# Linear attention and a gated MLP in one kernel: K and q of two steps transposed in 64x64 tiles, with a new order of all instructions

## The chip, the cores and the metric

One NeuronCore of a Trainium2 chip runs the whole program. The metric is the device time of one execution in microseconds (us); the median of several runs counts. The engines are TensorE (PE, with its weight loads listed apart as PEld), VectorE (DVE), ScalarE (ACT), GpSimd (POOL) and SyncE (SP, which here only issues DMAs). Each works through its own queue in order and waits on semaphores for the others.

## The reference

Two stages follow each other. The first is attention with a decay per head, in blocks of 64 positions, with a 64x64 state per head; the second is a gated MLP whose gate mixes positions.

```python
# q, k, v: (4, 8, 768, 64) float32; lam: (8,)
for b in range(12):                                   # blocks of 64 positions
    intra = (qb @ kb^T) * Dmask                       # Dmask[i, j] = lam ** (i - j) for i >= j, else 0
    out[:, :, sl] = intra @ vb + (qb * lam_pow) @ kv_state
    kv_state = lam ** 64 * kv_state + (kb * rev_pow)^T @ vb
x = out.transpose(0, 2, 1, 3).reshape(4, 768, 512)
h = relu(x @ w_in)                                    # w_in: (512, 1024)
u, v = h[..., :512], h[..., 512:]
v_n = (v - mean(v)) / sqrt(var(v) + 1e-6)             # over the 512 features
v_s = w_spatial @ v_n + b_spatial                     # over the 768 positions
y = (u * v_s) @ w_out                                 # (4, 768, 512) float32
```

## The kernel before

The work is cut into 12 steps; step n is 256 positions (two chunks c of 128) of batch n // 3, all 8 heads. The decay is put into k and q themselves: k is multiplied by lam to a power of the position (`lv`), q by the inverse power (`lqn`, or `lq` after the transpose), so the mask is of zeros and ones.

A step goes through these operations; each is a short function, and the name in brackets is its token in the order:

- loads of 512 KB each of q, k, v (LQ, LK, LV) on SP's queue; three buffers each (`q_in`, `k_in`, `v_in`), so the load of step n waits until step n-3 has used its buffer;
- k times its decay to bf16 (KM), q cast (QC) or scaled (QM), v cast (VC), into two buffers each (`kc`, `qc`, `vb`);
- the transposes of k and q, which the scores need with the 64 features on the partitions. Steps 0 to 4: on PE (TK, TQ: 128x128 tiles against an identity, eight for a whole step, into one PSUM bank), then a copy out of PSUM (EK) and a product with `lq` (EQ). Steps 5 to 11: DMA transposes on SP's queue (DK, DQ);
- scores (SC), the mask (MK, on DVE, the largest single group of DVE), the state (KV, or KS, which mixes the state's matmuls into half of the scores), the state's copy (SS), the product with v and the state (AV), the copy to `xT` (EX); SC, KV, KS and AV use 64x64 tiles of PE;
- the v half of w_in (PV), its relu (EV), the statistics (BN, RA, RD, NB), the normalised v (VN), the u half (PU) and its relu (EU); 128x128 tiles.

When the three steps of a batch are done, its gate follows: the bias is copied to a PSUM bank (GP), w_spatial times v_n is added (PW), the product with u is taken (GM), and w_out (PO, or PH for half of a tile's columns) gives the output, copied (EO, EH) and stored (ST, SH) by SP. w_spatial is transposed once on PE (WT, EW). The weights are loaded and cast by DMAs on POOL's queue: WI.0 and WI.1 (the v and the u half of w_in), WS.0 and WS.1 (w_spatial), WO (w_out). GT on POOL only reads one number of a load, so that what follows it on POOL waits for that load. FL are four matmuls of the identity with no result that is used; LB, LN, LL, LX and LT make the decays from `lam`.

PSUM has eight banks; bank 7 holds the state, the other seven are given out by the order. The order of everything is written out by hand in the string `ORDER`: each token is an operation, its arguments and its engine (T PE, D DVE, A ACT, P POOL, S SP). `TK.3.2.6.T` is the transpose of k of step 3, whole (2; 0 and 1 are halves), into bank 6. Each engine's queue is the tokens with its letter, in the order of the string, and semaphores are set for what reads and writes the same tile or bank:

```python
    with tc.manual_schedule():
        for token in ORDER.split():
            name, *args, e = token.split(".")
            ops[name](e, *map(int, args))
```

Lines of the profile: loads 192, KM and QM 286, casts and copies 177 (ACT), 179 (DVE), 181 (POOL), weights 248, 253 and 257, bias 260, GT 244, LN 210, LX 219 and 220, LT 224, TK and TQ 316, EQ 330, SC 347, MK 352, KV 364, KS 377 and 385, AV 406 and 415, PV 440, EV and EU 445 (ACT) and 447 (DVE), PU 488, WT 500, PW 514, GM 520, PO 525, PH 534, SH 544, ST 548, DMA transposes 299 (k) and 303 (q).

Of the kernel before, what the change touches and what calls it, by code (L numbers as in the profile page):

```python
# [21 lines left out]
FL.4.6.T MK.0.0.2.3.D TQ.2.0.2.T MK.1.1.0.1.D AV.0.0.3.6.T FN.0.3.6.A TQ.2.1.0.T SS.0.1.A MK.1.0.4.5.D LT.2.A
KM.2.0.P KV.1.0.T AV.1.0.1.4.T KM.2.1.D WS.1.P TK.2.0.5.T AV.0.1.3.6.T LV.2.S SS.1.0.D FN.1.1.4.A KV.1.1.T
LK.3.S EX.0.1.6.A AV.1.1.1.4.T BS.S LK.5.S EX.1.0.1.A EK.2.0.5.D LQ.3.S EX.0.0.3.D PV.0.1.5.T FL.15.6.T
EX.1.1.4.A WO.P TK.2.1.3.T GT.1.2.P PV.1.1.1.T EV.1.1.1.A EQ.2.1.0.D EQ.2.0.2.D VC.2.P WT.0.0.0.T EK.2.1.3.D
SC.2.0.2.3.T PV.1.0.4.T BN.1.1.D PV.0.0.6.T EW.0.0.0.A MK.2.0.2.3.D EV.0.1.5.A EV.1.0.4.A SC.2.1.0.1.T SS.1.1.A
PU.1.1.5.T BN.1.0.D WT.2.0.4.T KV.2.0.T MK.2.1.0.1.D RA.1.A BN.0.1.D LV.3.S AV.2.0.2.3.T EV.0.0.6.D SS.2.0.A
FN.2.2.3.D PU.1.0.0.T BN.0.0.D AV.2.1.2.3.T EX.2.1.3.D RD.1.D WT.1.0.1.T RA.0.A NB.1.D RD.0.D EX.2.0.2.A
EW.1.0.1.D EW.2.0.4.A NB.0.D VN.0.0.A WT.1.1.6.T KM.3.0.P EW.1.1.6.D KM.3.1.P VC.3.P WT.2.1.3.T PV.2.1.2.T
PV.2.0.1.T VN.1.0.A PU.2.1.4.T LK.4.S EV.2.0.1.A WT.0.1.6.T VN.1.1.A EV.2.1.2.D EU.1.0.0.A BN.2.0.D EU.1.1.5.A  # L30
BN.2.1.D VN.0.1.D LQ.4.S PU.2.0.2.T RA.2.A RD.2.D EW.0.1.6.A PU.0.0.1.T GP.0.0.0.0.A VN.2.1.D PU.0.1.5.T
# [5 lines left out]
GM.0.1.0.2.D EQ.4.2.5.D GM.0.0.1.1.D AV.3.0.3.6.T KM.5.1.P LK.6.S LV.5.S VC.4.A FN.3.3.6.D KS.4.0.4.5.T SS.4.0.A
GM.0.2.0.0.D SC.4.1.1.2.T AV.3.1.3.6.T KS.4.1.4.5.T QM.5.1.P PO.0.4.0.T QM.5.0.D MK.4.0.4.5.D EX.3.1.6.A
EX.3.0.3.A PO.0.5.6.T EO.0.4.0.A KM.6.0.D PV.3.0.3.T DK.5.S EV.3.0.3.A LQ.6.S MK.4.1.1.2.D PU.3.0.4.T PV.3.1.5.T
VC.5.P DQ.5.S KM.6.1.P GP.0.3.0.0.D PW.0.3.0.0.T QM.6.1.P AV.4.0.1.2.T SS.4.1.A EV.3.1.5.A LQ.7.S EO.0.5.6.A  # L40
BN.3.0.D FN.4.1.2.A DK.6.S LK.7.S EU.3.0.4.D LV.6.S QM.6.0.P KV.5.0.T SC.5.0.3.4.T SC.5.1.5.6.T AV.4.1.1.2.T
DQ.6.S GM.0.3.0.0.D EX.4.0.1.A PO.0.1.0.T PO.0.0.1.T SS.5.0.D MK.5.1.5.6.D MK.5.0.3.4.D LK.8.S EX.4.1.2.A
EO.0.0.1.D PV.4.0.5.T AV.5.0.2.6.T EV.4.0.5.A EO.0.1.0.D PV.4.1.3.T FN.5.2.6.D LQ.8.S EV.4.1.3.A AV.5.1.2.6.T
EX.5.1.6.A EX.5.0.2.A BN.3.1.D BN.4.0.D PO.0.3.4.T QM.7.0.P PU.4.1.1.T BN.4.1.D LV.7.S KM.7.0.P VC.6.D
PV.5.0.5.T RA.4.A EU.4.1.1.A PV.5.1.0.T KM.7.1.D PU.5.1.3.T RA.3.A RD.3.D EV.5.0.5.A RD.4.D EV.5.1.0.A BN.5.0.D
ST.0.1.S SC.6.1.1.2.T EO.0.3.4.A QM.7.1.P NB.3.D KS.6.0.5.6.T BN.5.1.D DK.7.S NB.4.D DQ.7.S PU.4.0.0.T SS.6.0.A
# [541 lines left out]
```

## Time and profile before

| | |
|---|---|
| time, median of 3 runs | 146.82 us (146.6 to 147.3) |
| the profiled execution | 147.23 us, its span 145.5 us |
| PE / PEld busy | 130.7 us (90%) / 84.2 us (58%) |
| DVE / ACT / POOL busy | 113.3 us (78%) / 81.1 us (56%) / 46.8 us (32%) |
| DMA | 32.28 MB, mean 222 GB/s over the span |
| chain that ended last | PE 61%, DMA 22%, POOL 4%, DVE 4% |

The span is what the profiler recorded from the first to the last instruction; the execution's own time is a little longer. Busy time of PE counts a matmul from its start to its modelled end, and matmuls overlap, so the cadence (start to start) is what a matmul costs when the next follows. The chain is followed back from the last instruction: at each step to what released it, or to the instruction before it on its engine. Rows of the timeline and of the chain give start, duration, engine, line of the program, operation and tiles; in brackets stands the idle time before and what ended it. Rows of the windows give for each stretch its length, the busy time and number of instructions of PE, PEld, DVE, ACT and POOL, the granted clock, the DMA share and GB/s.

### The profile page before, as it was taken

What the parts mean: (1) busy time and instruction counts of PE and PEld (TensorE: products, weight loads), DVE (VectorE), ACT (ScalarE), POOL (GpSimd) and SP (SyncE); (2) the same over time, 40 slices, a digit from 0 to 9 for tenths busy, and PEclk for the clock granted to TensorE, in tenths of its full rate; (3) what the DMA queues carried; (4) which work ended last, traced back from release to release, by engine and by line L of the source; (5) the groups of instructions that cost most, each with busy time, mean ns of one, the idle gap of its engine ahead of it and who ended that gap; (6) DMA issues with size and microseconds to landing.
All of it is one profiled execution on the core that took longest, in us unless ns stands there. A gap on an engine that the chain in (4) does not pass through costs nothing.

```text
span 145.5 us, 4623 instructions
## 1 busy us (share of the span) xinstructions
PE 130.7 (90%) x1938; PEld 84.2 (58%) x1954; DVE 113.3 (78%) x227; ACT 81.1 (56%) x161; POOL 46.8 (32%) x59
## 2 busy tenths in 40 slices
PE   1269999899999996999999999999999999999990
PEld 1147765578756655457765646766665644865630
DVE  2568975987899985978999988979789779877410
ACT  3775276669938553378954442979233235870151
POOL 7449910205058256331902494034110000000000
PEclk9999999999999999999999999999999999999999
DMA  3999999999999999999999999998933002715064
GB/s 88 346 347 347 228 214 216 216 236 335 295 250 347 220 202 264 299 192 358 176 299 179 347 343 248 192 330 257 192 83 138 5 0 93 272 75 213 0 258 177
DMA packets 58375, 32.28 MB, mean 222 GB/s; under 512 B 15858, under 2 KB 55282, under 8 KB 58354
## 3 DMA queue, kind: packets, MB, share of 16 engines
q1 hardware_dynamic: 55968, 29.23, 78.3%
q0 software_dynamic: 2384, 2.75, 10.8%
q8 instruction: 15, 0.25, 0.7%
q14 instruction: 6, 0.05, 0.1%
q10 hardware_dynamic: 2, 0.00, 0.0%
HBM read 24.77 MB, written 6.29 MB: 213 GB/s over the span
## 4 chain that ended last, share of the span: by engine, by line
PE 61%; DMA 22%; POOL 4%; DVE 4%; issue 2%; SPq 2%; ACT 2%; POOLq 0%
PE ps L514 17%; PE ps L525 13%; PE ps L488 11%; PE ps L440 10%; DMA k_in<-in_k_dram 9%; DMA win_sb<-in_moe_w_in_dram 8%; DMA qT<-qc 4%; PE ps L415 3%; PE ps L347 2%; SPq L192 2%; PE ps L406 2%; DVE a_sb L352 2%; POOL kc L286 2%; ACT vn L476 1%; POOL qc L181 1%
## 5 line engine op out<-in xcount | busy, mean ns | idle before, releaser
L514 PE MATMUL ps<-wt_sb,vn 128*128 128x384 bf16 x192 | 34.2, 326 | 0.0
L352 DVE TENSOR_TENSOR a_sb<-ps,m 128x1024 bf16<-128x1024 f32 x24 | 28.8, 1215 | 2.7 <-PE ps L406 1.3
L286 POOL TENSOR_TENSOR kc<-k_in,lv 128x512 bf16<-128x512 f32 x17 | 17.6, 1044 | 27.2 <-PE ps L377 11.7
L514 PEld LDWEIGHTS <-vn 128*128 128x128 bf16 x192 | 18.0, 98 | 11.5
L488 PE MATMUL ps<-xT,win_sb 128*128 128x256 bf16 x192 | 23.8, 273 | 0.8 <-DMA win_sb<-in_moe_w_in_dram 0.6
L440 PE MATMUL ps<-win_sb,xT 128*128 128x512 bf16 x91 | 22.9, 379 | 0.5 <-issue 0.2
L525 PE MATMUL ps<-wout_sb,gT 128*128 128x512 bf16 x81 | 21.3, 379 | 1.0 <-issue 0.5
L488 PEld LDWEIGHTS <-win_sb 128*128 128x128 bf16 x192 | 18.4, 98 | 5.5 <-DMA win_sb<-in_moe_w_in_dram 0.8
L520 DVE TENSOR_TENSOR gT<-ps,uT 128x384 bf16<-128x384 f32 x32 | 17.1, 549 | 4.3 <-PE ps L514 3.5
L455 DVE BATCH_NORM_STATS2 st<-vh 128x6 f32<-128x512 bf16 x24 | 16.3, 680 | 1.9 <-ACT vh L445 1.8
L177 ACT ACTIVATE o_sb<-ps 128x512 f32<-128x512 f32 (+1 forms) x19 | 10.7, 570 | 11.7 <-PE ps L525 11.2
L286 POOL TENSOR_TENSOR qc<-q_in,lqn 128x512 bf16<-128x512 f32 x12 | 12.4, 1046 | 11.8 <-DMA q_in<-in_q_dram 7.1
L445 ACT ACTIVATE vh<-ps 128x512 bf16<-128x512 f32 x17 | 10.1, 592 | 10.4 <-PE ps L440 10.3
L177 ACT ACTIVATE xT<-ps 128x512 bf16<-128x512 f32 x18 | 9.9, 596 | 9.7 <-PE ps L415 9.7
L440 PEld LDWEIGHTS <-xT 128*128 128x128 bf16 x96 | 8.9, 98 | 9.5 <-ACT xT L177 0.5
L525 PEld LDWEIGHTS <-gT 128*128 128x128 bf16 x92 | 8.4, 98 | 8.5
L181 POOL CAST vb<-v_in 128x1024 bf16<-128x1024 f32 x6 | 6.2, 1038 | 18.9 <-DMA v_in<-in_v_dram 13.7
L445 ACT ACTIVATE uT<-ps 128x512 bf16<-128x512 f32 x18 | 10.1, 592 | 0.9 <-PE ps L488 0.9
L415 PE MATMUL ps<-a_sb,vb 64*64 64x128 bf16 x384 | 10.5, 226 | 0.0
L177 ACT ACTIVATE ps<-bsp 128x384 f32<-128x384 f32 x18 | 8.6, 494 | 2.9 <-DVE a_sb L352 1.9
L347 PE MATMUL ps<-qT,kT 64*64 64x128 bf16 x288 | 8.2, 240 | 2.0 <-DMA qT<-qc 1.1
L476 ACT ACTIVATE vn<-vh,shift,rstd 128x512 bf16<-128x512 bf16 x11 | 8.5, 807 | 1.7 <-DVE shift L470 1.7
(77 smaller groups left out, 175.7 us busy)
## 6 DMA issues: line engine op xcount, KB each, us to landing
q_in<-in_q_dram SPq DMA_DIRECT2D x12, 512.0 KB, 6.0
k_in<-in_k_dram SPq DMA_DIRECT2D x12, 512.0 KB, 6.0
v_in<-in_v_dram SPq DMA_DIRECT2D x12, 512.0 KB, 6.0
out_dram<-o_sb SPq DMA_DIRECT2D x23, 256.0 KB, 2.4
wsp_raw<-in_moe_w_spatial_dram POOLq DMA_DIRECT2D x2, 576.0 KB, 12.8
win_sb<-in_moe_w_in_dram POOLq DMA_DIRECT2D x2, 512.0 KB, 10.8
wout_sb<-in_moe_w_out_dram POOLq DMA_DIRECT2D x1, 512.0 KB, 17.8
bsp<-in_moe_b_spatial_dram SPq DMA_DIRECT2D x1, 384.0 KB, 21.4
```

What stands on the lines that cost most here:

```text
L177: nc.scalar.activation(out=o, in_=i, func=AF.Copy)
L286: vec(e).tensor_tensor(out=dst[n % NCA][:, u].rearrange("p u m o d -> p o (u m) d"), in0=src[n % NIN].rearrange("p (o u) m d -> p o u m d" ...
L347: nc.tensor.matmul(out=pa[o][row(c), w, j], lhsT=kT[n % NTR][row(o), u, j, c * Q64:(c + 1) * Q64], rhs=qv(n, o, u, c), start=(w == 0 and j ...
L352: nc.vector.tensor_tensor(out=a_sb[n % NA][:, i].rearrange("p o w j x -> p o w (j x)"), in0=ps[:, b0:b1 + 1:b1 - b0].rearrange("p o (w y) ...
L415: nc.tensor.matmul(out=po[c ^ o][row(w), c, i], lhsT=vb[n % NCA][row(c), 4 * o + u, j, :], rhs=a[row(c), i, o, w, j, :], start=(r == 0 and ...
L440: nc.tensor.matmul(out=bank(b), lhsT=x[:, slot(c, g)], rhs=win_sb[:, g, DH:DFF], start=(g == 0), stop=(g == NCH - 1))
L445: nc.scalar.activation(out=o, in_=i, func=AF.Relu)
L455: nc.vector.bn_stats(out=st6[p2][:, t], in_=vh[p2][:, t])
L488: nc.tensor.matmul(out=pu[:, f2].rearrange("p (c x) -> p c x", c=2), lhsT=win_sb[:, g, f * P:(f + 1) * P], rhs=x[:, slot(0, g):slot(1, g) ...
L514: nc.tensor.matmul(out=bank(b)[:, 0:HW], lhsT=vn[bb % 2][:, s, f * P:(f + 1) * P], rhs=wt_sb[:, s, i * HW:(i + 1) * HW], start=False, stop ...
L520: nc.vector.tensor_tensor(out=gT[bb % 2][:, f, cols], in0=bank(b)[:, 0:HW], in1=uT[bb % 2][:, f, cols], op=ALU.mult)
L525: nc.tensor.matmul(out=bank(b), lhsT=gT[bb % 2][:, f, t * P:(t + 1) * P], rhs=wout_sb[:, f, :], start=(f == 0), stop=(f == NCH - 1))
```

## The change

K and q of steps 3 and 4 are transposed by one operation, TT, instead of TK and TQ: 64 transposes of 64x64 tiles, k first and then q. A tile of rows c goes to the first or second of two neighbouring banks, k to the first half of each bank, q to the second. FK copies k out of both banks with one instruction, FQ multiplies q out of both with `lq`. Steps 0 to 2 keep TK and TQ in halves, steps 5 to 11 the DMA transposes.

The order string is another one throughout: every queue has a new sequence, many operations another bank, some another engine (GP 26 on ACT and 6 on DVE, where 18 and 14 were; VN 8 and 16, where 11 and 13 were). There are three FL instead of two. The two half tiles of the output (PH, EH, SH) come after all other output tiles.

```diff
-LQ.0.S lam.A msk.P idn.P LK.0.S LQ.1.S mkc.D QC.0.1.D posk.P pos.P LB.0.T LN.0.A LL.D QC.0.0.P LK.1.S LX.A
-KM.0.1.D QC.1.0.D TQ.0.0.1.T KM.0.0.D LT.1.A LT.0.A TK.0.1.2.T TQ.0.1.3.T EQ.0.1.3.D KM.1.1.D TK.0.0.4.T LV.0.S
-KM.1.0.P EK.0.1.2.A EQ.0.0.1.D WI.0.P EK.0.0.4.D SC.0.1.5.6.T QC.1.1.P WS.0.P TQ.1.0.0.T LV.1.S VC.0.A
...
+pos.P msk.P lam.A LQ.1.S QC.1.0.A idn.P LK.0.S posk.P LK.1.S LQ.0.S QC.0.1.P LV.0.S GT.1.1.P mkc.D LB.0.T VC.0.P
+LN.0.A WI.0.P FL.16.1.T TQ.1.0.2.T LV.1.S QC.1.1.D LL.D LX.A LT.0.A FL.0.3.T KM.0.0.D TK.0.0.4.T EK.0.0.4.A
+KM.1.0.D TK.1.0.5.T KM.0.1.D TK.0.1.6.T EK.1.0.5.A TQ.1.1.1.T QC.0.0.D EK.0.1.6.A KM.1.1.D TQ.0.0.0.T TQ.0.1.3.T
+TK.1.1.4.T EQ.0.1.3.D SC.0.1.5.6.T EK.1.1.4.D LT.1.A EQ.1.1.1.D EQ.0.0.0.D KV.0.0.T SS.0.0.D LQ.2.S MK.0.1.5.6.D
+KV.0.1.T GT.1.2.P WS.0.P WI.1.P GT.2.1.P SC.0.0.3.4.T QC.2.1.P VC.1.A QC.2.0.A LK.2.S SS.0.1.A KM.2.1.P
...
+AV.1.1.3.4.T LV.2.S EX.1.1.4.A VC.2.P KV.2.0.T SC.2.0.5.6.T EX.1.0.3.D MK.2.0.5.6.D SS.2.0.D LK.3.S LQ.3.S
+PV.1.0.2.T PV.1.1.0.T EV.1.1.0.D SC.2.1.3.4.T MK.2.1.3.4.D PV.0.1.1.T BS.S EV.0.1.1.D WT.1.0.5.T WT.0.0.6.T
+PV.0.0.0.T AV.2.0.3.4.T BN.1.1.D WO.P PU.1.1.1.T LQ.4.S KM.3.1.P EW.1.0.5.A FN.2.3.4.D AV.2.1.3.4.T QC.3.2.P
...
-EU.0.1.5.A TK.3.2.6.T GP.0.2.1.5.A VN.2.0.D EU.0.0.1.A PW.0.0.0.0.T EW.2.1.3.D GT.2.1.P QC.3.2.D EU.2.1.4.A
-LV.4.S EK.3.2.6.D PW.0.2.1.5.T GP.0.1.1.1.A GM.0.0.0.0.D GP.0.3.1.4.A GP.0.2.0.0.A TQ.3.2.3.T PW.0.1.1.1.T
...
-MK.3.0.5.6.D TK.4.2.3.T KM.5.0.P GM.0.3.1.4.D PW.0.1.0.2.T LQ.5.S EK.4.2.3.A TQ.4.2.5.T PW.0.0.1.1.T
...
+WT.2.1.6.T EW.1.1.4.A EU.1.0.5.A RA.2.A PU.2.0.3.T EU.2.0.3.A TT.3.4.5.T EW.2.1.6.D VN.1.0.A VN.0.1.D
+GP.0.2.1.3.A RD.2.D EU.0.0.2.A VN.2.0.D VN.0.0.D VN.2.1.D KM.4.0.P EU.0.1.0.D PU.2.1.6.T EU.2.1.6.D GP.0.0.0.0.A
+PW.0.2.1.3.T PW.0.0.0.0.T FQ.3.4.5.D QC.4.2.D FK.3.4.5.A SC.3.1.4.5.T EU.1.1.1.A GM.0.2.1.3.D KS.3.0.1.2.T
+GP.0.1.1.6.A PW.0.1.1.6.T SS.3.0.D GP.0.3.1.3.A MK.3.1.4.5.D GT.2.2.P GM.0.1.1.6.D KS.3.1.1.2.T KM.5.0.P
...
+PW.0.1.0.4.T TT.4.1.2.T FK.4.1.2.A GM.0.1.0.4.D FQ.4.1.2.D LQ.5.S QM.5.0.P VC.4.A QM.5.1.P PW.0.2.0.5.T
...
-PO.3.3.6.T ST.2.1.S GM.3.0.0.0.D EH.3.5.1.4.A EH.3.5.0.5.A ST.3.4.S SH.3.5.0.S GM.3.1.0.1.D PO.3.1.2.T
-PO.3.2.0.T SH.3.5.1.S EO.3.3.6.A ST.3.3.S EO.3.1.2.A ST.3.1.S EO.3.2.0.D PO.3.0.1.T ST.3.2.S EO.3.0.1.A ST.3.0.S
...
+ST.2.5.S PO.3.2.0.T PO.3.1.3.T EO.3.2.0.D ST.3.2.S PO.3.0.6.T EO.3.1.3.D ST.3.1.S PH.3.5.0.1.T EO.3.0.6.A
+ST.3.0.S PH.3.5.1.4.T EH.3.5.1.4.D EH.3.5.0.1.A SH.3.5.0.S SH.3.5.1.S
...
+    def pair(b0, b1, k):
+        return ps[:, b0:b1 + 1:b1 - b0].bitcast(BF16)[:, :, 512 * k:512 * k + 512].rearrange("p c (f y) -> p c f y", y=Q64)
+
+    def both(t):
+        return t.rearrange("p u m (c y) -> p c (u m) y", c=2)
+
+    def t_t(e, n, b0, b1):
+        for k, src in enumerate((kc, qc)):
+            bk = [bank(b).bitcast(BF16)[:, 512 * k:512 * k + 512].rearrange("p (u m y) -> p u m y", u=4, m=2) for b in (b0, b1)]
+            for u in range(4):
+                for m in range(2):
+                    for o in range(2):
+                        for c in range(2):
+                            nc.tensor.transpose(out=bk[c][row(o), u, m], in_=src[n % NCA][row(c), u, m, o],
+                                                identity=ident[row(c), row(c)])
+
+    def f_k(e, n, b0, b1):
+        copy(e, both(kT[n % NTR]), pair(b0, b1, 0))
+
+    def f_q(e, n, b0, b1):
+        nc.vector.tensor_tensor(out=both(qT[n % NTR]), in0=pair(b0, b1, 1), in1=both(lq[:, n % NR]), op=ALU.mult)
```

More of the change, by code (lines that the diff above doesn't have):

```diff
@@ L22 @@
[L22 to L31, printed above, removed]
@@ L37 @@
[L37 to L46, printed above, removed]
```

89 lines of the change are left out of this document (51 added, 38 removed).

## The prediction

> **What bounds the kernel now.** I read the page's busy shares first, then the chain of work that ended last in order of time, then the timeline of the stretches where that chain leaves TensorE (PE).
>
> ```profile
> span 145.5 us, 4623 instructions
> PE 130.7 (90%) x1938; PEld 84.2 (58%) x1954; DVE 113.3 (78%) x227; ACT 81.1 (56%) x161; POOL 46.8 (32%) x59
> ...
> 14.74 12.27 DMA win_sb<-in_moe_w_in_dram
> 27.06 1.05 PE ps L488 x8
> ...
> 50.13 6.12 DMA qT<-qc
> 56.29 0.64 PE ps L347 x32
> ...
> 138.28 3.47 PE ps L525 x16
> 141.77 0.60 ACT o_sb L177
> ```
>
> From 27 us to 141.8 us the chain is nearly all PE. It leaves PE twice for something long: until 27.06 for the half of w_in that the u projections (PU) need, and until 56.25 for the DMA transpose of q of step 5. So between those points the time is the number of PE instructions times their cadence plus what PE waits, and the change can win or lose in four places only: the time of the first PU, PE's own work, PE's waits, and the last 3.8 us. The waits, grouped by who waited, say how little there is to win after 27 us:
>
> ```profile
> PE ps L347 <- DMA qT<-qc: 1.1, 1, 1.1
> PE ps L488 <- DMA win_sb<-in_moe_w_in_dram: 0.6, 1, 0.6
> SPq L303 <- DVE qc L286: 4.7, 1, 4.7
> ```
>
> **The opening: +1.45 us.** These rows of the timeline carry it:
>
> ```profile
> 2.88 0.80 POOL L203 IOTA posqi<- 128x768 int32 x1
> 3.56 0.18 ACT L210 ACTIVATE loglam<-ps 128x8 f32<-128x8 f32 x1 [0.93 <-PE ps L207]
> 3.76 1.28 ACT L219 ACT_TABLE_LOAD   x1
> 4.76 0.43 DVE L179 CAST qc<-q_in 128x512 bf16<-128x512 f32 x1 [1.88 <-DMA q_in<-in_q_dram]
> 6.34 0.69 DVE L286 TENSOR_TENSOR kc<-k_in,lv 128x512 bf16<-128x512 f32 x1 [0.37 <-ACT lv L220]
> 10.41 0.93 POOL L248 DMA_DIRECT2D win_sb<-in_moe_w_in_dram  x1
> 10.81 1.06 ACT L177 ACTIVATE vb<-v_in 128x1024 bf16<-128x1024 f32 x1 [0.87 <-DMA v_in<-in_v_dram]
> 12.65 1.05 POOL L181 CAST vb<-v_in 128x1024 bf16<-128x1024 f32 x1
> 14.71 3.49 DVE L352 TENSOR_TENSOR a_sb<-ps,m 128x1024 bf16<-128x1024 f32 x3
> 25.44 1.04 POOL L181 CAST vb<-v_in 128x1024 bf16<-128x1024 f32 x1 [6.61 <-DMA v_in<-in_v_dram]
> ...
> 8.00:12.00 4.00, 2.74 (x34) 1.86 (x32) 3.32 (x8) 3.00 (x6) 2.58 (x4) 1.00 1.15 347
> 12.00:16.00 4.00, 3.68 (x90) 2.98 (x90) 3.52 (x7) 0.87 (x2) 3.83 (x6) 1.00 1.18 307
> 20.00:24.00 4.00, 3.80 (x90) 2.39 (x86) 1.89 (x6) 2.31 (x5) 0.00 (x0) 1.00 1.18 218
> ```
>
> Two chains lead to the first PU, and both become later. The weights: POOL's queue now has VC.0 (the cast of v of step 0) ahead of WI.0. V0 is the fifth load in both orders and was there at 10.81; the cast takes 1.05 on POOL; so WI.0 is issued at about 11.87 in place of 10.41, +1.46. Behind it come WS.0 and WI.1 as before, so WI.1's half, which released PU at 27.0, should land at about 28.5.
>
> The other chain is K of step 0. On ACT the copy QC.1.0 now stands ahead of LN (Ln of lambda): it waits for the first load (4.76) and takes about 0.59, so LN starts at 5.35 in place of 3.56 (that `pos` with its iota of 0.80 and cast now precedes `msk` on POOL hides under this). Then Ln 0.18, the Exp table 1.28 and two Exp of 0.24: the first KM on DVE starts at about 7.3 in place of 6.34. Ahead of the last mask of step 1, DVE has 0.95 us more to do than before (two KM more at 0.68 and an SS at 0.41, against one QC of 0.43 and one net kT copy of 0.41 fewer), so that mask ends at about 20.2 in place of 14.71 + 3.49 = 18.2. Six small DVE jobs (3.0 us) later both halves of xT of step 1 exist, at 23.2. PE then has four PV, SC, two WT and an AV before the first PU: 3.45 + 0.35 + 0.7 + 0.45 + 0.2 is 5.15, so 28.4. The two chains meet; I take 28.5, +1.45 on 27.06. Lower bound 0 (the weights no later), upper bound +3 (first two PV at the slow early cadence as well, in which four transposes took the 0.61 us that eight take later).
>
> **What is already done by then: -0.9 us.** Ahead of the first PU the new order has one KV, one AV and one WT more than the old.
>
> ```profile
> 28.11 0.34 PE ps L500 x6
> 46.03 0.45 PE ps L316 x8
> 56.93 0.11 PE ps L406 x8
> 74.34 0.23 PE ps L406 x8
> 74.57 0.22 PE ps L415 x16
> 86.47 0.97 PE ps L525 x4
> 110.36 0.86 PE ps L525 x4
> 112.44 0.18 PE ps L364 x12
> ```
>
> WT is 0.34, KV 16 x 15 ns = 0.24, AV 0.11 + 0.22 = 0.33; together 0.9.
>
> **64x64 transposes: -0.8 us.** Removed in steps 3 and 4: 16 transposes each at 0.45 / 8 = 56 ns, 0.90 per step. Added: 64 each. No row shows a 64x64 transpose. The L415 rows, 64x64 tiles in all four corners with 128 columns, run at 14 ns each, so half the columns may run at 7; the L364 rows have 64 columns but use two corners at a time, 15 ns. That gives 0.45 to 0.96 per step. TT walks all four corners, so it is nearer to L415: I take 8 ns, 0.5, and gain 0.4 a step, -0.8 (bounds -0.9 and +0.1).
>
> **Changes between 64x64 and 128x128 work: +1.1 us.** Eight L406 matmuls cost 0.11 inside a run of 64x64 work and 0.23 after 128x128 work; four L525 cost 0.86 and, after 64x64 work, 0.97. Each change of tile size costs about 0.11. Counted in the two orders from the first PU on, there are 49 such changes before and 59 after (TT alone makes four, since both stand between PU or PW): +1.1. The Trainium skill has the rule behind this (TensorEngine Tiling (Array Packing), Key Properties): changing the tiling mode, not just the tile, drains TensorE; the trace agrees with the 0.11 above. Without the rule, by instruction count alone, this part would be 0.
>
> **Evacuation: 0.** FK and FQ move as much as EK and EQ did:
>
> ```profile
> L330 DVE TENSOR_TENSOR qT<-ps,lq 128x1024 bf16<-128x1024 bf16 x2 | 1.4, 681 | 0.0
> L177 ACT ACTIVATE kT<-ps 128x1024 bf16<-128x1024 bf16 x1 | 1.0, 1017 | 0.0
> L177 ACT ACTIVATE ps<-bsp 128x384 f32<-128x384 f32 x18 | 8.6, 494 | 2.9 <-DVE a_sb L352 1.9
> ```
>
> **Waits around steps 3 to 5: -1.1 + 0.8 us.** The wait at 56 us: q of step 5 is now scaled wholly on POOL, straight behind k, where before its second half was on DVE until 49.2 and SP waited 4.7 us for it. LQ.5 is the 17th load in both orders; two POOL passes of 1.04 after its landing bring the transpose to about 49.3 in place of 50.13, so it lands at 55.4, and PE, which now has AV.4.1 ahead of SC.5, should find it there: -1.1. Against that, TT.3 waits for k and q together, and QC.3.2 has gone from DVE to POOL. ACT then has VN, a GP, EU, a second GP and FK in one line: PW.0.0.0.0 and SC.3.1 stand behind them on PE, about one GP (0.5), and PW.0.1.1.6 behind an EU and a GP, about 0.3: +0.8 (0 to 2).
>
> **The end: -0.6 us.**
>
> ```profile
> out_dram<-o_sb SPq DMA_DIRECT2D x23, 256.0 KB, 2.4
> out_dram<-o_sb SPq DMA_DIRECT2D x2, 128.0 KB, 1.7
> ...
> 138.31 0.66 ACT L177 ACTIVATE o_sb<-ps 128x256 f32<-128x256 f32 x2 [0.28 <-PE ps L534]
> 139.90 2.83 SPq L548 DMA_DIRECT2D out_dram<-o_sb  x4
> ```
>
> The PE work is the same. The last copy falls from 0.60 to about 0.4 and the last store from 2.4 to 1.7, but three stores now leave SP within 0.8 us, so part is paid again: -0.6 (-0.2 to -0.9).
>
> **The rest, 57 to 136 us: +0.5 us.** The loads, DMA transposes and masks of steps 6 to 11 keep a slack of over 1 us against PE wherever I set the two orders side by side; the old order has only some 0.3 us of such waits there. For a new order I take 0.5 (0 to 2).
>
> Sum: 1.45 - 0.9 - 0.8 + 1.1 - 1.1 + 0.8 - 0.6 + 0.5 = +0.45. The profiled execution took 147.23 us (145.5 of span), 0.4 above the median of the three runs (146.82). It becomes 147.7, and a median of **147.3**.
>
> **The rivals.**
>
> *v of step 2 starves (slower).* Weights and loads share the DMA engines: 347 GB/s up to 12 us, 218 after, and by the 307 between, the weights set in near 14.7, 4.3 us after WI.0's issue. V2, the ninth load, would at 347 GB/s (1.51 us each, the first down at 4.7) have come at 16.8; it came at 25.44. The 1.4 loads left at 14.7 took 10.7 us, so they crept at near 0.07 MB per us, a fifth of the speed. With the weights setting in at 11.87 + 4.3 = 16.2 only 0.4 of a load is left, V2 comes near 19.3 and its cast ends near 20.4. But KV.2.0 now stands ahead of all PV in PE's queue and is due near 22.5: if the weights set in before 15.7, the cast is later than that, and PE and everything behind wait. Half a microsecond earlier, at 15.2, the wait is 2: **149.3**. Against it: the same delay from issue gives 16.2. Chance 0.17.
>
> *A table load between QC.1.0 and Ln (slower).* Ln is ACT's first function now and its table load hides under the start. A copy ahead of it may put the load behind that copy: 1.28 us more on the K chain, the first PU at 29.7: **148.5**. For it: the second function, Exp, loads a table too. Chance 0.17.
>
> *The opening is not later, or made up (faster).* If the weights' stream starts as early as before relative to the loads yet V2 is in time, or PE's waits of +0.8 and +0.5 do not come, -1.3 to -2.7 remain of the sum: PE is the bound from 27 us on and the cuts at 56 us and at the end are in the chain. About **145.4**. For it: PE's row is full. Chance 0.27.
>
> *The pair of banks serialises (slower).* FK on ACT and FQ on DVE now read the same two banks; before, K and q lay in different banks. If one follows the other, SC.3.1 and KS.4.0 come 0.7 later each, at most, and the transposes stay at 15 ns: 147.3 + 0.9 gives **148.2**. The Trainium skill (PSUM — Partial Sum Buffer, PSUM bank collisions) holds that two engines may not read one bank and quadrant at once; no run here shows such a pair. Chance 0.07.
>
> **How the numbers follow.** The forecast's own case has 0.32, from 146.2 to 148.2. A measurement of this kernel tells about 0.5% (0.73 us) from no change, so the forecast lies inside that; its case gives 0.07 faster, 0.14 same, 0.11 slower. The faster rival gives 0.25 and 0.02 same, the slower three 0.39 and 0.02 same: 0.32 faster, 0.18 same, 0.50 slower. The range, 145.0 to 149.6, takes in all five and leaves the ends of the first and third rival out.
>
> **What would show it.** Right: the first L488 matmul near 28.5 with a short wait on win_sb; TT's 64 matmuls within 0.5 us; no PE wait on qT at step 5; last store landing within 2.8 us of PE's end. Wrong: a table load on ACT after 5 us; a PE wait before the KV of step 2; more than 2 us of PE waits between 57 and 136 us.

## The result, and the profile after

The changed kernel takes 148.63 us (median; 148.56 to 150.24) against 147.06 for the kernel before on the same chip: a ratio of 1.013 with a 95% interval of 1.0085 to 1.0176. It is slower by 1.3%. The forecast was 147.3; what came is the second rival's case, a table load ahead of Ln, priced at 148.5.

The profiled execution took 148.68 us (before 147.23). The page of the changed kernel:

```profile
span 147.0 us, 4834 instructions
PE 132.4 (90%) x2054; PEld 84.0 (57%) x2054; DVE 114.6 (78%) x228; ACT 78.8 (54%) x158; POOL 48.5 (33%) x60
```

PE is as full as before; it starts to be so later. The code has moved 22 lines down behind line 333: PU is L510, SC L369, KS L399 and L407, AV L428 and L437, PV L462, MK L374, PW L536, PO L547, and TT is L347, FQ L354. PE's waits in the changed kernel, who waited for whom, us in total, times, longest:

```profile
PE ps L207 <- DVE one_row L241: 4.7, 1, 4.7
PE ps L316 <- DVE kc L286: 3.4, 2, 3.0
PE ps L369 <- DVE qT L330: 0.6, 2, 0.4
...
PE ps L536 <- ACT ps L177: 0.4, 2, 0.2
PE ps L369 <- ACT kT L177: 0.3, 1, 0.3
```

The waits for win_sb and for the DMA transpose of q of step 5, on which the old chain turned, are gone. In their place PE waits longer in the opening, 3.0 us for the first K (0.8 at most before). ACT's first table load in the kernel before is this one:

```profile
1.35 1.28 ACT L210 ACT_TABLE_LOAD   x1 [1.35 <-PEq L572]
```

The timeline of ACT, DVE and PE in the changed kernel's opening says what has changed (start, duration, engine, line, operation):

```profile
1.34 1.28 ACT L177 ACT_TABLE_LOAD   x1 [1.34 <-PEq L594]
...
4.90 0.63 ACT L177 ACTIVATE qc<-q_in 128x512 bf16<-128x512 f32 x1 [2.28 <-DMA q_in<-in_q_dram]
...
5.55 1.28 ACT L210 ACT_TABLE_LOAD   x1
...
6.84 0.18 ACT L210 ACTIVATE loglam<-ps 128x8 f32<-128x8 f32 x1
7.04 1.28 ACT L219 ACT_TABLE_LOAD   x1
...
8.88 1.74 DVE L286 TENSOR_TENSOR kc<-k_in,lv 128x512 bf16<-128x512 f32 x2 [1.29 <-ACT lv L220]
...
25.41 1.90 PE L462 MATMUL ps<-win_sb,xT 128*128 128x512 bf16 x8 [0.51 <-DVE xT L179]
...
30.55 0.83 PE L510 MATMUL ps<-xT,win_sb 128*128 128x256 bf16 x6
```

Before, the load at the start belonged to Ln (L210). Now the copy QC.1.0 (L177) is ACT's first function; a table is loaded for it at the start, and Ln, which follows, gets another: 1.28 us in the open. The first KM starts at 8.88 instead of 6.34, the first PU at 30.55 instead of 27.06. From there on the changed kernel is quicker. The two stretches behind the first PU, cut at the scores of step 5, in the windows of the kernel before and then of the changed kernel (length, then busy time and instructions of PE, PEld, DVE, ACT, POOL, granted clock, DMA share, GB/s):

```profile
27.06:56.25 29.19, 27.93 (x460) 19.61 (x463) 25.23 (x51) 18.88 (x36) 11.19 (x13) 1.00 1.12 262
56.25:141.75 85.50, 84.05 (x1151) 51.67 (x1163) 70.06 (x141) 45.27 (x92) 20.80 (x21) 1.00 0.79 200
```

```profile
30.55:58.35 27.80, 27.14 (x537) 17.86 (x532) 25.55 (x54) 17.84 (x34) 12.82 (x13) 1.00 1.07 275
58.35:143.37 85.02, 85.00 (x1160) 51.28 (x1150) 67.86 (x137) 44.52 (x93) 21.79 (x21) 1.00 0.79 190
```

It wins 1.4 us in the first and 0.5 us in the second, where PE does not stand at all any more. The second stretch also holds less work: AV.4.1 (0.33 us) now stands ahead of the scores of step 5. And the 1.45 us by which PE's busy time falls short of that stretch before are mostly no waiting: the page of before has 91 and 81 matmuls of PV and PO against 96 and 92 of their weight loads, and the gaps stand where these 16 records are missing. In e9 below, which has the old order there and all records, PE is busy 85.34 of 85.50 us. From PE's end to the end of the span it is 3.60 instead of 3.77. So: +3.5 in the opening, -1.9 behind it, -0.2 in the tail. The ratios leave out executions more than 1.5% above the fastest of the same kernel (one of e3 took 176.4 us); the profiled one of e6 is among them, so its profile is not read.

### The profile page after: what moved, and what is told of

The parts are those of the page before. It is cut to its first block, busy times and chain, and to the rows that moved or that the text cites. A ratio compares the mean times of both kernels' runs of the same rounds, so it can differ in the third digit from the quotient of the medians.

```text
span 147.0 us, 4834 instructions
## 1 busy us (share of the span) xinstructions
PE 132.4 (90%) x2054; PEld 84.0 (57%) x2054; DVE 114.6 (78%) x228; ACT 78.8 (54%) x158; POOL 48.5 (33%) x60
## 3 DMA queue, kind: packets, MB, share of 16 engines
q1 hardware_dynamic: 55968, 29.23, 77.7%
## 4 chain that ended last, share of the span: by engine, by line
PE 78%; DVE 9%; ACT 6%; DMA 3%; issue 1%; DVEq 0%; ACTq 0%
PE ps L536 21%; PE ps L547 14%; PE ps L462 14%; PE ps L510 12%; PE ps L437 5%; PE ps L369 3%; PE ps L428 3%; DMA q_in<-in_q_dram 3%; PE ps L316 2%; DVE a_sb L374 2%; DVE kc L286 2%; PE ps L386 1%; PE ps L407 1%; DVE vn L501 1%; PE ps L399 1%; DVE st L477 1%
## 5 line engine op out<-in xcount | busy, mean ns | idle before, releaser
L536 PE MATMUL ps<-wt_sb,vn 128*128 128x384 bf16 x192 | 34.4, 327 | 0.4 <-ACT ps L177 0.4
L374 DVE TENSOR_TENSOR a_sb<-ps,m 128x1024 bf16<-128x1024 f32 x24 | 28.8, 1216 | 2.5 <-PE ps L369 2.0
L286 POOL TENSOR_TENSOR kc<-k_in,lv 128x512 bf16<-128x512 f32 x16 | 17.0, 1071 | 25.6 <-DVE a_sb L374 7.7
L536 PEld LDWEIGHTS <-vn 128*128 128x128 bf16 x192 | 17.8, 98 | 12.5 <-issue 0.5
L462 PE MATMUL ps<-win_sb,xT 128*128 128x512 bf16 x96 | 23.9, 380 | 0.5 <-DVE xT L179 0.5
L510 PE MATMUL ps<-xT,win_sb 128*128 128x256 bf16 x192 | 24.1, 273 | 0.0
L547 PE MATMUL ps<-wout_sb,gT 128*128 128x512 bf16 x92 | 22.0, 379 | 0.0
L510 PEld LDWEIGHTS <-win_sb 128*128 128x128 bf16 x192 | 18.2, 98 | 4.6
L177 ACT ACTIVATE xT<-ps 128x512 bf16<-128x512 f32 x18 | 10.1, 593 | 9.6 <-PE ps L437 9.6
L177 ACT ACTIVATE ps<-bsp 128x384 f32<-128x384 f32 x26 | 12.6, 492 | 4.5 <-DVE a_sb L374 2.5
L467 ACT ACTIVATE vh<-ps 128x512 bf16<-128x512 f32 x14 | 8.3, 596 | 11.8 <-PE ps L462 9.6
L177 ACT ACTIVATE o_sb<-ps 128x512 f32<-128x512 f32 (+1 forms) x14 | 7.9, 578 | 12.4 <-PE ps L547 12.4
L181 POOL CAST vb<-v_in 128x1024 bf16<-128x1024 f32 x9 | 9.4, 1049 | 14.2 <-PE ps L437 8.5
L462 PEld LDWEIGHTS <-xT 128*128 128x128 bf16 x96 | 8.6, 98 | 9.6 <-DVE xT L179 0.7
L547 PEld LDWEIGHTS <-gT 128*128 128x128 bf16 x92 | 8.7, 98 | 8.9
L286 POOL TENSOR_TENSOR qc<-q_in,lqn 128x512 bf16<-128x512 f32 x11 | 11.8, 1085 | 5.3 <-DMA q_in<-in_q_dram 3.1
L437 PE MATMUL ps<-a_sb,vb 64*64 64x128 bf16 x384 | 10.5, 228 | 0.5 <-DVE a_sb L374 0.5
L179 DVE COPY o_sb<-ps 128x512 f32<-128x512 f32 (+1 forms) x11 | 7.1, 657 | 3.6 <-PE ps L547 2.4
L369 PE MATMUL ps<-qT,kT 64*64 64x128 bf16 x288 | 8.3, 239 | 0.8 <-DVE qT L330 0.6
```

What stands on the lines that cost most here:

```text
L177: nc.scalar.activation(out=o, in_=i, func=AF.Copy)
L286: vec(e).tensor_tensor(out=dst[n % NCA][:, u].rearrange("p u m o d -> p o (u m) d"), in0=src[n % NIN].rearrange("p (o u) m d -> p o u m d" ...
L369: nc.tensor.matmul(out=pa[o][row(c), w, j], lhsT=kT[n % NTR][row(o), u, j, c * Q64:(c + 1) * Q64], rhs=qv(n, o, u, c), start=(w == 0 and j ...
L374: nc.vector.tensor_tensor(out=a_sb[n % NA][:, i].rearrange("p o w j x -> p o w (j x)"), in0=ps[:, b0:b1 + 1:b1 - b0].rearrange("p o (w y) ...
L437: nc.tensor.matmul(out=po[c ^ o][row(w), c, i], lhsT=vb[n % NCA][row(c), 4 * o + u, j, :], rhs=a[row(c), i, o, w, j, :], start=(r == 0 and ...
L462: nc.tensor.matmul(out=bank(b), lhsT=x[:, slot(c, g)], rhs=win_sb[:, g, DH:DFF], start=(g == 0), stop=(g == NCH - 1))
```

## The experiments

The theory at the start: the opening, and in it the copy ahead of Ln, costs more than the whole slowdown. Its rivals: the pairs of banks and the tile-size changes cost it; or the first PU is set by the weights anyway. This table has the stretches of each profile, in us, from the starts of PE's matmuls, and the ratio of each kernel to the kernel before.

| kernel | first PU | to SC of step 5 | to PE's end | ratio to the kernel before (95%) |
|---|---|---|---|---|
| before | 27.06 | 29.23 | 85.44 | 1 |
| changed | 30.55 | 27.82 | 84.98 | 1.013 (1.0085 to 1.0176) |
| e1, QC.1.0 on DVE | 28.97 | 28.61 | 84.98 | 1.0044 (1.0017 to 1.0071) |
| e2, and POOL's start as before | 28.82 | 27.83 | 84.98 | 1.0056 (1.0031 to 1.0080) |
| e5, old order with the copy ahead of Ln | 28.86 | 30.10 | 85.21 | 1.0123 (1.0078 to 1.0168) |
| e3, old order with TT | 27.37 | 30.17 | 85.49 | 1.0078 (1.0053 to 1.0103) |
| e9, e3 with FK on DVE | 27.10 | 28.80 | 85.50 | 1.0001 (0.9983 to 1.0018) |
| e4, new order without TT | 30.19 | 27.56 | 84.98 | 1.0095 (1.0060 to 1.0130) |
| e8, e2 without TT | 29.34 | 27.70 | 84.98 | 1.0064 (1.0052 to 1.0076) |
| e7, the kernel before with more FL | 26.96 | 28.60 | 85.43 | 1.0002 (0.9979 to 1.0025) |
| e10, old opening, new rest | 26.84 | 32.55 | 84.98 | 1.0202 (1.0170 to 1.0233) |
| e12, e10 with FK on DVE | 27.24 | 31.53 | 86.28 | 1.0213 (1.0176 to 1.0250) |
| e13, e10 with its seam mended | 27.00 | 31.59 | 84.98 | 1.0154 (1.0124 to 1.0183) |

The stretches are of one execution each, the ratios of many. The profiled execution of e2 took 147.09 us, 0.9 below the median of its runs, that of e5 149.63, 0.6 above. And e4 has the changed kernel's opening, e8 that of e2, but their first PU comes 0.36 earlier and 0.52 later: differences of half a microsecond between two rows say little.

**e5: the suspected harm alone, in the old order.**

```diff
-LQ.0.S lam.A msk.P idn.P LK.0.S LQ.1.S mkc.D QC.0.1.D posk.P pos.P LB.0.T LN.0.A LL.D
+LQ.0.S lam.A msk.P idn.P LK.0.S LQ.1.S mkc.D QC.0.1.A posk.P pos.P LB.0.T LN.0.A LL.D
```

> The kernel before with one edit: the cast of the second half of q of step 0 (QC.0.1) goes from DVE to ACT, ahead of Ln: the suspected harm of the new order's opening alone. Theory A: a second table load of 1.28 us appears on ACT ahead of Ln, the first KM starts at about 8.3 to 8.9 us instead of 6.34, and if the opening's K chain sets the first PU, that comes 1 to 2 us later and the time rises by 0.8 to 1.8 us, to 147.7 to 148.6. Rival C (the old order's first PU waits for the u half of w_in until 26.7 us and had 0.6 us of waiting in hand): the table load is there, the first KM is as late, but the time rises by at most 0.9 us.

Measured: 148.99 us, a ratio of 1.0123 (1.0078 to 1.0168): one letter in the old order costs as much as the whole change did, 1.8 us, the upper end of theory A and twice what rival C allowed. ACT's timeline in this kernel:

```profile
4.83 0.63 ACT L177 ACTIVATE qc<-q_in 128x512 bf16<-128x512 f32 x1 [2.21 <-DMA q_in<-in_q_dram]
5.48 1.28 ACT L210 ACT_TABLE_LOAD   x1
6.77 0.18 ACT L210 ACTIVATE loglam<-ps 128x8 f32<-128x8 f32 x1
6.97 1.28 ACT L219 ACT_TABLE_LOAD   x1
```

The same rows as in the changed kernel; the first KM starts at 8.81, 2.5 us late, the first PU is 1.8 us late, and no wait for win_sb is left. The 0.6 us that PE waited for the weights before was all that the delay could hide in. Shown: this copy ahead of Ln costs about 1.2% by itself.

**e1 and e2: the harm undone in the new order.**

```diff
-pos.P msk.P lam.A LQ.1.S QC.1.0.A idn.P LK.0.S posk.P LK.1.S LQ.0.S
+pos.P msk.P lam.A LQ.1.S idn.P LK.0.S posk.P LK.1.S LQ.0.S               (e1)
+msk.P lam.A LQ.1.S idn.P LK.0.S posk.P LK.1.S pos.P LQ.0.S               (e2)
-LN.0.A WI.0.P FL.16.1.T TQ.1.0.2.T
+LN.0.A WI.0.P FL.16.1.T QC.1.0.D TQ.1.0.2.T                              (both)
```

> The new kernel with one edit: the cast of the first half of q of step 1 (QC.1.0) goes from ACT back to DVE, so that Ln is ACT's first function. Theory A (the opening: the copy on ACT ahead of Ln costs a second table load, and the whole K chain, the first full PE work and PE's full clock come late): Ln no longer has a table load of 1.28 us ahead of it, the first KM on DVE starts at about 7.4 us instead of 8.88, the first PU at 28.6 to 29.3 instead of 30.61, and the time falls by 1.2 to 2.0 us, to about 147.0. Rival B (the opening only hands its delay to waits that come later anyway; the slowdown sits in the pairs of banks, the tile-size changes and the tail): the first PU may come earlier, but the time falls by under 0.5 us, to 148.2 or more. Rival C (weights): the first PU cannot come before the u half of w_in lands at about 28.3, so PE shows a wait of over 0.5 us for it.

> As the run before, and in addition POOL makes the mask and the identity first and the positions of q (pos) after the positions of k, as the kernel before did. Theory A: one_row is ready about 1 us earlier, Ln starts at about 4.3, the first KM at 6.4; the first PU is then bounded by the u half of w_in at about 28.3 to 28.5, as the prediction had it for both chains; the time is 146.2 to 146.8, about 2 us under the new kernel and 0.2 to 0.8 under the kernel before. Rival B: within 0.5 us of the new kernel. Rival C: no gain over the run before, since the weights bind there already.

Measured: 147.96 and 147.95 us. The second table load is gone in both, and the ratio falls from 1.013 to about 1.005, so more than half of the slowdown goes with it. By the ratios e1 gains 1.3 us, the low end of theory A's 1.2 to 2.0; the 146.2 to 146.8 that it promised for e2 did not come. Rival C had e2 right, no gain over e1, but not for its reason: PE waits for the weights in neither.

What is left of the slowdown is only in part in the table. In e1 the first PU comes 1.6 us earlier than in the changed kernel, but 0.8 us of this is lost again behind it, where PE waits 0.7 us for kT and 0.4 for the normalised v. e2's profile loses nothing there, but it is of a quick execution. In both the first PU is still 1.8 to 1.9 us behind the old one, although in e2 the first KM starts at 6.67, with the old one's 6.34 almost reached. Two rows from the chain of e2 say why an earlier Ln gave no more, and then one thing that delays its opening:

```profile
1.94 6.13 DMA k_in<-in_k_dram
8.09 0.70 DVE kc L286
...
15.95 1.58 DVE kc L286
```

The second load of k lands at 8.07 and releases the second KM, however early Ln is. KM of step 2 then takes 1.58 us on DVE, while POOL casts q and multiplies k beside it; in the changed kernel, with only a DMA issue on POOL, it takes 0.68:

```profile
18.12 0.68 DVE L286 TENSOR_TENSOR kc<-k_in,lv 128x512 bf16<-128x512 f32 x1
```

The new order also puts more behind the first KM (two KM and an SS more ahead of the last mask of step 1), and in e1 PE runs at half speed for longer. How much each of these weighs was not tried. The windows of e1 at the clock's own steps:

```profile
8.67:12.08 3.41, 3.25 (x38) 2.84 (x41) 2.80 (x5) 3.40 (x8) 2.74 (x4) 1.00 1.15 346
12.08:15.49 3.41, 1.56 (x76) 1.13 (x69) 3.39 (x7) 2.00 (x4) 1.98 (x4) 1.00 1.15 347
15.49:18.91 3.42, 2.36 (x68) 1.92 (x71) 2.72 (x4) 0.23 (x2) 3.31 (x5) 0.50 1.20 245
18.91:22.32 3.41, 3.41 (x74) 2.97 (x66) 2.79 (x5) 2.54 (x7) 1.76 (x2) 0.50 1.16 218
22.32:25.70 3.38, 3.00 (x71) 1.59 (x72) 2.91 (x6) 0.60 (x1) 0.00 (x0) 1.00 1.18 216
```

The granted clock is the 1.00 or 0.50 behind POOL's share (1.00 also where no record of it exists yet, as in the first row). It changes in steps of 3.41 us: here it was full after a stretch in which PE was busy 3.25 of 3.41, half after one with 1.56, full again after one without a gap. In the kernel before the record of full speed begins at 20.0 us, in the changed kernel at 23.4, in e2 at 21.0. Four matmuls of FL took 0.61 us at 5.18 us in the changed kernel and 0.40 at 23.55.

**e6 and e7: filling PE's gaps in the opening with FL**, to bring the full clock on earlier (e6 adds 13 to e2, e7 adds 9 to the kernel before).

```diff
-LN.0.A WI.0.P FL.16.1.T QC.1.0.D TQ.1.0.2.T                              (e6)
+LN.0.A WI.0.P FL.16.1.T FL.0.5.T FL.0.6.T FL.0.5.T QC.1.0.D TQ.1.0.2.T
...
-KM.0.1.D QC.1.0.D TQ.0.0.1.T                                             (e7)
+KM.0.1.D QC.1.0.D FL.0.5.T FL.0.6.T FL.0.5.T FL.0.6.T TQ.0.0.1.T
...
```

> The kernel of the run e2 (new order, QC.1.0 on DVE, POOL's old start) with 13 more FL (four matmuls of the identity each, no result used) put where PE waited between 4 and 17.6 us. Theory D (clock): the granted clock of PE came on at full rate only at a window edge, 21.0 us in the profile of e2, 23.4 in the new kernel, 20.0 before; which window it is depends on how gapless PE's work is and on the phase of the windows, and this spreads e2's runs from 147.0 to 148.3. With the gaps filled the full clock begins by 12 us, the small matmuls and transposes of 12 to 21 us run at half their time, and the median falls to 147.0 to 147.4. Rival E: that stretch is bound by DVE (3.3 to 4.0 of every 4 us busy) and by the weights, the clock there costs nothing: the median stays at 147.7 to 148.2, or rises where a filler delays a transpose.

> The kernel before with 9 more FL put where its PE waited between 3.5 and 10 us. Theory D: the full clock comes on before 20.0 us, and the median falls from 146.95 to about 146.5, the fastest runs of the kernel before, with less spread. Rival E: no change, 146.9 to 147.1, since the first PU waits for the u half of w_in at 26.7 us in any case.

Measured: e7 146.57 us (146.79 for the kernel before on that chip), a ratio of 1.0002 (0.9979 to 1.0025): no change that can be told, as rival E said. The full clock did come on at 7.8 us, but it went again at 14.6 and came back at 21.4. e6 did not get quicker: a ratio of 1.0085 (1.0056 to 1.0115), which overlaps that of e2. Its times spread from 147.6 to 152.7 us, and why is not known. So whether an earlier full clock alone would help the new order is not settled; fillers were no way to get it.

**e3 and e9: TT alone in the old order**, with FK on ACT, and then on DVE beside FQ.

```diff
-EU.0.1.5.A TK.3.2.6.T GP.0.2.1.5.A ... EK.3.2.6.D ... TQ.3.2.3.T ... EQ.3.2.3.D
+EU.0.1.5.A GP.0.2.1.5.A ... TT.3.3.6.T ... FQ.3.3.6.D FK.3.3.6.A          (e9: FK.3.3.6.D)
-TK.4.2.3.T ... EK.4.2.3.A TQ.4.2.5.T ... EQ.4.2.5.D
+TT.4.3.5.T ... FK.4.3.5.A FQ.4.3.5.D                                       (e9: FK.4.3.5.D)
```

> The kernel before, with its own order, and only the transposes of steps 3 and 4 changed: TT, FK (ACT) and FQ (DVE) in the places of TQ, EQ and EK, into banks 3 and 6, and 3 and 5. The prediction's price for this part alone: PE -0.4 us a step, -0.8 together, four tile-size changes more at 0.11 each (+0.44), so 146.7 against 147.06. Theory A with the trace of the new kernel: the same -0.4, and up to 0.4 us a step back where FK waits for FQ, or FQ for FK, at the same banks and SC waits for the later of the two: 146.6 to 147.2, no difference that can be told. Rival B (the pairs are what costs): 147.8 or more, and PE waits of over 0.5 us a step for kT or qT.

> The kernel of the run e3 (old order, TT for steps 3 and 4) with one edit: FK goes from ACT to DVE, next to FQ, so that the two readers of one pair of banks stand on one engine and neither waits for the other's semaphore. Theory F (what TT costs in the old order is the wait of the second reader for the first, 0.94 us of idle DVE ahead of FQ in step 4, then 0.79 us of PE for qT, and ACT's FK behind FQ and a line of GP in step 3): the waits for kT and qT fall under 0.5 us together and the time to 147.0 to 147.4. Rival G (the 64x64 transposes or the reads of two banks themselves cost): it stays at 148.0 or more.

Measured: e3 148.25 us (ratio 1.0078), e9 146.84 (1.0001). e3 refutes what theory A expected of it. Rival B was right that the change costs, and e9 narrows down what in it does. From e3, PE's waits from 36 to 58 us, then FK of step 3 on ACT and FQ of step 4 on DVE; after them PE's waits of e9 in the same stretch:

```profile
PE ps L407 <- ACT kT L177: 0.9, 1, 0.9
PE ps L437 <- DVE qT L354: 0.8, 1, 0.8
```

```profile
42.04 1.02 ACT L177 ACTIVATE kT<-ps 128x1024 bf16<-128x1024 bf16 x1
...
49.34 0.69 DVE L354 TENSOR_TENSOR qT<-ps,lq 128x1024 bf16<-128x1024 bf16 x1 [0.94 <-ACT kT L177]
```

```profile
PE ps L407 <- DVE kT L179: 0.4, 1, 0.4
PE ps L437 <- DVE qT L354: 0.3, 1, 0.3
```

In step 4 FQ stands idle for 0.94 us until FK on ACT is done with the same two banks, and AV of step 3, which writes bank 3 of this pair, waits 0.8 behind it. In step 3 FK starts at 42.04, when FQ (to 42.01) and a relu ahead of it on ACT (to 42.08) are both done, and KS (L407) stands 0.9 us until the copy is there. In e9 the two readers still follow each other, but FK takes 0.68 us on DVE instead of 1.02 on ACT. The two waits fall from 1.7 to 0.7 us (theory F had under 0.5), and the whole 0.8% goes. So TT itself costs nothing that can be measured, and wins nothing either. Shown is that FK's place on ACT costs; how much of this is the turn-taking of two engines at one pair of banks, how much the slower copy and how much ACT's queue, no run separates. (The old order had the copy of step 3 on DVE too.)

**e4 and e8: TT undone in the new order**, in the changed kernel and in e2.

```diff
-TT.3.4.5.T ... FQ.3.4.5.D QC.4.2.D FK.3.4.5.A
+TK.3.2.4.T TQ.3.2.5.T ... EQ.3.2.5.D QC.4.2.D EK.3.2.4.A
-TT.4.1.2.T FK.4.1.2.A GM.0.1.0.4.D FQ.4.1.2.D
+TK.4.2.1.T TQ.4.2.2.T EK.4.2.1.A GM.0.1.0.4.D EQ.4.2.2.D
```

> The new kernel with its new order, and only TT undone: k and q of steps 3 and 4 by TK and TQ in 128x128 tiles, each into one bank of the same pair, EK on ACT and EQ on DVE. Theory A: eight transposes of 128 columns cost 0.45 for each of k and q instead of 0.55 for both by 64x64, so PE +0.35 a step, less two tile-size changes a step at 0.11; EK no longer waits for EQ, up to -0.4 us in step 3: the time is 148.3 to 149.1, so this part of the change is within 0.5 us of nothing. Rival B: the time falls by 1 us or more, to 147.6 or less.

> The kernel of the run e2 with TT undone as in the run e4 (TK and TQ, EK on ACT and EQ on DVE, each with a bank of its own). If the two parts add up (opening -0.7 us, TT -0.35 us against the new kernel), the time is 147.5 to 147.7, and its first PU to SC.5 is 27.6 us against 27.8 with TT. If PE's first-PU time binds everything and TT's waits were hidden, 147.95 as e2.

Measured: 148.29 us and 147.73 us, each within the interval of the kernel it is made from. From the first PU to step 5 they are 0.26 and 0.13 us shorter, less than the openings of two profiles of one order differ (0.36 and 0.52). FK in step 3 of the changed kernel and EK in its place in e4, on ACT:

```profile
41.87 1.02 ACT L177 ACTIVATE kT<-ps 128x1024 bf16<-128x1024 bf16 x1 [0.48 <-DVE qT L354]
```

```profile
40.96 1.02 ACT L177 ACTIVATE kT<-ps 128x1024 bf16<-128x1024 bf16 x1
```

FK waited 0.48 for FQ; EK, with a bank of its own, for nobody. In the new order most of that wait is hidden: PE waited 0.3 us for kT.

**e10, e12, e13: the old opening with the new rest.** The string is the old one up to the scores of step 2 (113 tokens) and from there the new one without what is done by then. e12 has FK on DVE; e13 mends the seam.

```diff
+... EV.1.0.4.A SC.2.1.0.5.T SS.1.1.A | GT.2.1.P PU.1.1.1.T KV.2.0.T SS.2.0.D MK.2.1.0.5.D WT.1.0.2.T AV.2.0.3.4.T ...   (e10)
+... EV.1.0.4.A SC.2.1.4.5.T SS.1.1.A | GT.2.1.P EV.0.0.6.A BN.0.1.D PU.1.1.1.T KV.2.0.T MK.2.1.4.5.D BN.1.0.D SS.2.0.D WT.1.0.0.T AV.2.0.3.4.T ...   (e13)
```

> The old order up to the scores of step 2 (all of the opening, 113 tokens, ahead of the first PU), and from there the new order with everything that is then still to do, TT, FK and FQ of steps 3 and 4 included; the scores of half of step 2 and one w_spatial transpose got other banks so that the first PU can follow at once. Theory A (the new order loses 3.5 us in the opening and wins about 2 us behind it): first PU at 27.0 as before, then 112.8 us of PE as in the new kernel plus 0.9 us of work that the new kernel had done by then, PE's end at 140.8 and the time at 145.8 to 146.4, under both kernels. Rival H (what the new order wins behind the first PU is only the echo of its late start: weights, loads and DVE had time to run ahead): with the early start the waits come back and the time is 146.8 or more.

> The kernel of the run e10 with FK of steps 3 and 4 on DVE, behind FQ in step 3 and ahead of it in step 4, so that neither reader of the pair waits for the other engine. Theory F: the PE waits around SC.3.1 and KS.4.0 for kT and qT fall by 0.3 to 0.6 us together and the time is 0.2 to 0.6 us under the run e10. Rival: DVE is the tighter engine there (3.3 to 4.0 of every 4 us busy between 28 and 48 us), FK's two times 0.7 us push the masks and gates back, and the time is that of e10 or more.

> The kernel of the run e10 with its seam mended: the scores of half of step 2 go to banks 4 and 5 and the w_spatial transpose behind the first PU to bank 0 (in the run e10 that transpose waited 1.72 us for a mask, and DVE had stood 2.65 us behind a state copy ahead of that mask), and the mask stands on DVE ahead of the state copy. Theory A: no such wait is left, PE's clock does not fall back at 30.8 us, SC.3.1 follows 13.3 us after the first PU, at about 40.4, and the rest runs as in the new kernel (15.4 us to SC.5, 85.0 to PE's end): PE ends at 140.8 and the time is 145.8 to 146.5, below both kernels. Rival H (what the new order wins behind its first PU is the echo of the late start): DVE and ACT do not keep up from 27 to 41 us, SC.3.1 comes at 41.4 or later, and the time is 146.8 or more.

Measured: 149.91, 150.08 and 149.09 us; all three are slower than the kernel before and none is quicker than the changed one, so theory A's 145.8 to 146.5 is refuted. So is theory F for the new order: with FK on DVE, which took the whole 0.8% away in the old one, e12 is no quicker than e10. The first PU does come at 26.8 to 27.2. In e10 PE then waits 1.72 us at the seam, and in the next step of the clock it has half its speed (windows of e10):

```profile
27.40:30.81 3.41, 1.69 (x51) 1.34 (x49) 1.56 (x2) 0.30 (x1) 0.00 (x0) 1.00 1.17 216
30.81:34.22 3.41, 3.16 (x49) 2.37 (x39) 2.46 (x7) 3.11 (x5) 0.57 (x1) 0.50 1.15 285
```

e13 has neither, and shows what the late start had hidden. On POOL and PE:

```profile
36.74 0.45 PE L347 MATMUL ps<-ident,kc 64*64 64x64 bf16 x32
38.16 1.03 POOL L181 CAST qc<-q_in 128x1024 bf16<-128x1024 f32 x1 [2.73 <-DMA q_in<-in_q_dram]
39.24 0.45 PE L347 MATMUL ps<-ident,qc 64*64 64x64 bf16 x32 [2.06 <-POOL qc L181]
```

PE reaches TT of step 3 at 36.74, 2.0 us earlier than in the changed kernel (38.70), transposes k and stands 2.06 us for q, whose load only landed when POOL's cast starts, at 38.16. SC of step 3 starts at 43.16, in the changed kernel at 42.95. The 3.5 us won in front are gone by then. That fits rival H: part of the gain behind the first PU is there because PE came late and the loads did not. It does not prove it. The splice has a harm of its own: in the old opening a load of k of step 5 stands ahead of q of step 3 on SP, and its 512 KB at the 296 to 311 GB/s from 31 to 39 us make some 1.7 us of the 2.06 (an estimate). And the other runs are divided: e1 loses half of what it wins in front, e2's profile has its first PU 1.7 us ahead of the changed kernel's and the same 27.8 us behind it. An order that brings both the early PU and an early q of step 3 was not tried, so whether one beats the kernel before stays open. No run beat both kernels; e7 and e9 equal the kernel before.

## Why the prediction was right or wrong

- **The opening, +1.45: the step that failed.** Measured +3.49. The forecast let Ln start right behind the copy and put the table load between them into a rival with 0.17. It is there, 1.28 us, and with it the first KM starts at 8.88 where 7.3 was forecast. From KM to the first PV another 0.6 us came on top (16.5 us instead of 15.9), from there to the first PU 5.14 as forecast (5.15). PE had no wait for the weights left that could hide any of it. e5 shows the load by itself (1.0123), e1 its removal (1.013 to 1.0044). It is not the whole error: without it e1 still has its first PU 1.9 us behind the old one.
- **v of step 2 starves, a rival with 0.17.** It did not: the cast of v of step 2 starts on POOL at 21.21, and what it waited for was AV on PE, not the load.
- **Work done before the first PU, -0.9; waits around steps 3 to 5, -1.1 + 0.8; the rest, +0.5.** Together with the two PE terms they were to give -0.4 between the first PU and PE's end; measured -1.87 (114.67 to 112.80). The wait for q of step 5 went as forecast. PE's waits between 40 and 44 us came to 0.7, near the 0.8. The rest was mis-sized: PE is busy 85.00 of 85.02 us where 0.5 us of new waits was forecast, and the old order had about 0.2 to lose there (e9). With these three as measured and the other terms as forecast the sum is about -1.2; for some 0.7 us of the -1.87 there is no term.
- **64x64 transposes, -0.8.** The size came. TT of step 3 in the changed kernel:

```profile
38.70 0.45 PE L347 MATMUL ps<-ident,kc 64*64 64x64 bf16 x32
38.98 0.43 PE L347 MATMUL ps<-ident,qc 64*64 64x64 bf16 x32
39.34 1.05 PE L510 MATMUL ps<-xT,win_sb 128*128 128x256 bf16 x8
```

  The 32 of k take 0.28 us from start to start, 9 ns each, where 8 were forecast; the 0.64 to the next matmul holds a change of tile size, which the forecast prices apart. The 16 large ones take 0.89 in e4. In the time nothing shows (e9).
- **The pair of banks serialises, a rival with 0.07.** That one reader waits for the other is real: FQ 0.94 us behind FK in e3, FK 0.48 behind FQ in the changed kernel. At its price of 0.9 it did not come: PE waited 0.3 us for kT there, and e4, without the pairs, is 0.35% lower, within the interval. What FK on ACT costs in the old order is 0.8%.
- **Changes of tile size, +1.1.** 48 before and 58 after, counted in the traces from the first PU on (49 and 59 in the forecast). Their price can be read there: at 24 of 24 changes from 128x128 to 64x64 tiles before, and at 28 of 29 after, the next matmul starts 0.09 us later than the cadence of the ones before it. That is near the 0.11; no run changes their number alone.
- **The end, -0.6.** Measured -0.17 (3.77 to 3.60). That is what the last copy won (0.60 to 0.42 us). From its end to the end of the span it is 3.1 us, as before, where the forecast had 0.7 less for the smaller store; why is open.

The sign was right, and 148.6 lies in the range, but not by the forecast's own case: the opening was 2.0 us too low, the stretch behind it 1.5 us too high, the tail 0.4 too low. The largest error had been written down as a rival at nearly the right price; that its 148.5 came so close is partly luck, since it had the first PU at 29.7, where 30.55 came, and too little won behind it.

## What to carry to other kernels

Before moving work to ScalarE at the start of a kernel, look at which function comes first on it: a copy ahead of the first Ln cost a table load on the critical chain, and one letter in the old order made 1.2%. When two engines evacuate one pair of PSUM banks, read them as a chain: the second waits for the first, and what writes the banks next waits for both. Putting both on one engine took 0.8% away in the old order and nothing in the new one, so look first at whether PE waits there. And a stretch that gets quicker behind a late start is no gain in hand: test it with the start on time before adding the two up.
